# Weight pieces and converted blocks beside a linear attention, two turns later

## The chip, the core and the metric

The kernel runs on one core of a Trainium2 chip. The metric is the device time of one execution in microseconds, as a median of several runs. A core has five engines that each take their own instructions in order: TensorE (PE; its weight loads are listed as PEld), VectorE (DVE), ScalarE (ACT), GpSimd (POOL) and SyncE (SP), which here issues the loads and stores. They meet by semaphores: an instruction that waits holds everything behind it on its engine.

## The reference

Three layers follow one another; the sizes are batch 4, 8 heads, 768 tokens, head size 64. The first is a linear attention with decay in blocks, with a state that is carried from block to block:

```python
intra = np.einsum('bhic,bhjc->bhij', qb, kb) * Dmask[None]
intra = np.einsum('bhij,bhjd->bhid', intra, vb)
inter = np.einsum('bhid,bhde->bhie', qb * lam_pow[None], kv_state)
out[:, :, sl] = intra + inter
kb_dec = kb * rev_pow[None]
kv_state = lam_block[None, :, None, None] * kv_state + np.einsum('bhsd,bhse->bhde', kb_dec, vb)
```

The second is a soft mixture of 8 experts with 4 slots each: logits `x @ phi`, a softmax over all 3072 tokens that gathers the slots' inputs, `relu(slot @ w1[e]) @ w2[e]` for each expert (w1 512 x 1024, w2 1024 x 512, in float32), and a softmax over the slots that hands the results back. The third is a dense layer whose weights come as float64:

```python
h = x @ w_in
g = h * (1.0 / (1.0 + np.exp(-1.702 * h)))
return (g @ w_out).astype(np.float32)
```

## The kernel before, in words

**Turns.** The attention is cut into 32 steps: 4 batches, 2 halves of 384 tokens, 4 pairs of heads. A loop runs `for i in range(-2, NSTEP)`, and its order of instructions is the order on each engine, written out by hand. Turn i works on several steps at once: the scores of step i+1 (`do_SC`, tile bs, L293; VectorE multiplies them by the decay, L296), the transposes of q and k of step i+2 (`do_T`, tiles bq and bk, copied by ScalarE to qT, L265, and kT, L268), the transposes of the result of step i-1 (`do_XT`, tile bt, L351), the states' part of the result (`do_XS`, bx, L332), the state updates of step i+1 (`do_ST`, bst by TensorE at L306, then sa and s3 by VectorE at L315 and L317), the decayed k of step i+2 (`do_kd`, L281) and the rest of the result (`do_XA`, L340, copied by ScalarE to xT, L343). Then come the loads, and last GpSimd's product qdT of step i+2 (`do_qd`, L274). The step's updates are two or three pairs, for the last half of a batch has one chunk less. Beside each group of four turns stands the softmax tail of the group before (lines 360 to 473), so the turns differ in length. In this text turn i of the trace begins with the scores that the loop issues in turn i.

**Buffers.** qT and kT have one buffer each, but for a few steps at the ends. So the copy into qT of a step waits until the scores and GpSimd's product of the step before have read it.

**Expert pieces.** The first 32 pieces of w1 and w2, of 512 KB, are loaded beside the attention by `load_pieces(i)` (DMA issues at L155 and L157), the others after it as pieces are used up. All of these loads, those of q, k and v too, stand in SP's one queue in the order of the program.

**Blocks of float64.** Ten blocks of w_in and w_out, 128 x 256 numbers of 8 bytes, are turned into float32 beside the attention: `load_early(c)` loads block c into the only buffer `stage` (L221), and `do_early(c)` converts it: absolute values by ScalarE (L176), three bit operations by VectorE (L185, L188, L191), and two operations by GpSimd (L198, L199), of which the second reads what the third of VectorE leaves. EVERY is 2, so a block is loaded and one converted in every second turn.

**After the attention** come the experts (to about 194 us of the span) and a long stage of matrix products (bo, L986) to the end.

Of the kernel before, what the change touches and what calls it, by code (L numbers as in the profile page):

```python
# [17 lines left out]
def attention_moe_gelu_kernel(  # L18
# [31 lines left out]
    NSTEP = NG * NHP  # L50
    NE = 1
    NPC = 32
# [55 lines left out]
    def step_of(s):  # L108
        g, hp = divmod(s, NHP)
        b, hf = divmod(g, NHF)  # L110
        return b, hf, hp, g

    def load_step(s, what="qkv"):
        if s >= NSTEP:
            return
        b, hf, hp, g = step_of(s)
        t0 = hf * HS
        if "q" in what:

            q_r[s] = early.tile([P, 2, R * D], F32, tag="qr", name="qr", bufs=3)  # L120
            SP.dma_start(out=q_r[s], in_=q[b, 2 * hp:2 * hp + 2, t0:t0 + HS, :].rearrange("h (p c) d -> p h (c d)", p=P))
        for src, nm, ts, bufs, pool in ((k, "k", k_t, 3, early), (v, "v", v_t, 3, attn)):
            if nm in what:
                t = pool.tile([P, R, 2, D], F32, tag=nm, name=nm, bufs=bufs)
                for h in range(2):
                    SP.dma_start(out=t[:, :, h, :],
                                 in_=src[b, 2 * hp + h, t0:t0 + HS, :].rearrange("(c p) d -> p c d", p=P))
                ts[s] = t
# [17 lines left out]
    def load_piece(t=None):  # L146
        n = nxt_w[0]
        if n >= len(wlist):
            return
        nxt_w[0] += 1  # L150
        kind, e, j = wlist[n]
        if t is None:
            t = piece_room(n)
        if kind == "w1":
            SP.dma_start(out=t, in_=w1[e, j * P:(j + 1) * P, :])  # L155
        else:
            SP.dma_start(out=t.rearrange("p (k f) -> p k f", f=DM),  # L157
                         in_=w2[e, j * 2 * P:(j + 1) * 2 * P, :].rearrange("(k p) f -> p k f", p=P))
        w_pc[kind, e, j] = t
# [12 lines left out]
    def convert_abs(key, mask=None):  # L172
        if mask is None:
            mask = ex.tile([P, DM], F32, tag="cvm", name="cvm", bufs=3)
        m = mask
        ACT.activation(out=m, in_=staged[key][:, :, 1].bitcast(F32), func=AF.Abs)  # L176
        magn[key] = m

    def conversion(key, out, guard):


        t, m = staged.pop(key), magn.pop(key)
        up, low = t[:, :, 1], t[:, :, 0]
        a = out.bitcast(U32) if key[0] != "early" else stage[:, 2 * CB:3 * CB]
        DVE.tensor_scalar(out=a, in0=up, scalar1=3, scalar2=0x3FFFFFFF,  # L185
                          op0=ALU.logical_shift_left, op1=ALU.bitwise_and)
        yield
        DVE.scalar_tensor_tensor(out=a, in0=up, scalar=0xC0000000, in1=a,  # L188
                                 op0=ALU.bitwise_and, op1=ALU.bitwise_or)
        yield  # L190
        DVE.scalar_tensor_tensor(out=a, in0=low, scalar=29, in1=a,  # L191
                                 op0=ALU.logical_shift_right, op1=ALU.bitwise_or)
        yield
        if guard is DVE:
            DVE.scalar_tensor_tensor(out=out, in0=m, scalar=F64_MIN, in1=a.bitcast(F32),
                                     op0=ALU.is_ge, op1=ALU.mult)
        else:
            POOL.tensor_scalar(out=m, in0=m, scalar1=F64_MIN, scalar2=None, op0=ALU.is_ge)  # L198
            POOL.tensor_tensor(out=out, in0=a.bitcast(F32), in1=m, op=ALU.mult)  # L199

    def by_turns(*work, rounds=9):

        work = list(work)
        while work and rounds:
            work = [w for w in work if next(w, 0) is None]
            rounds -= 1
        return work
# [6 lines left out]
    EARLY = [(w_in32, kk * P, n * 512 + h * CB, w_in_sb[n][:, kk, h * CB:(h + 1) * CB])  # L214
             for n in range(NE) for kk in range(KD) for h in range(NCW)]
    EARLY += [(w_out32, 0, h * CB, wo[0][:, h * CB:(h + 1) * CB]) for h in range(NCW)]
    EVERY = (NSTEP - 8) // len(EARLY)
# [6 lines left out]
    def do_early(c):  # L224
        o = EARLY[c][-1]
        convert_abs(("early", c), o)
        by_turns(conversion(("early", c), o, POOL))
# [49 lines left out]
    def do_kd(s):  # L277
        b, hf, hp, g = step_of(s)
        t = early.tile([P, R, 2, D], F32, tag="kd", name="kd", bufs=1)
        for h in range(2):  # L280
            ACT.activation(out=t[:, :, h, :], in_=k_t[s][:, :, h, :], func=AF.Copy,  # L281
                           scale=dec[:, 2 * hp + h, P - 1:P])
        kd[s] = t
# [191 lines left out]
    with tc.manual_schedule():  # L475
# [7 lines left out]
        def warm_up(n):  # L483
            for _ in range(n):
                PE.matmul(bwarm, warm[:, :P], warm, start=True, stop=True)
# [17 lines left out]
        n = 1  # L503
# [12 lines left out]
        def make_isum():  # L516
            for j in range(G):
                for i in range(G):
                    POOL.tensor_copy(out=isum4[i * NS:(i + 1) * NS, j, :],
                                     in_=ident[i * NS:(i + 1) * NS, i * NS:(i + 1) * NS])  # L520

        def load_pieces(i):
            n = min(NPC, (i + 3) * NPC // NSTEP, NPC - 1 if i < NSTEP - 5 else NPC)
            while nxt_w[0] < n:
                load_piece()

        for i in range(-2, NSTEP):
            g, ph = divmod(i, NHP)
            if i > -2:
                load_step(i + 5, "q")  # L530
            if i == 1:
                make_isum()

            if 0 <= i + 1 < NSTEP:
                do_SC(i + 1)
            if 0 < i + 2 < NHP:

                for h in range(2):
                    make_dec(2 * (i + 2) + h)

            if 0 <= i + 2 < NSTEP:
                do_T(i + 2)
                if i == -2:
                    warm_up(1)
            if 0 <= i - 1 < NSTEP:
                do_XT(i - 1)
            if 0 <= i + 3 < NSTEP:
                do_q(i + 3)
            if ph == 1 and 0 <= g - 1 < NG:
                tail_L(g - 1)  # L550
            if ph == 2 and 0 <= g - 1 < NG:
                tail_max(g - 1)
            if ph == 3 and 0 <= g - 1 < NG:
                tail_exp(g - 1)
            if i == NSTEP - 1:
                tail_logits_first(NG - 1)
            if 0 <= i < NSTEP:
                do_XS(i)

            if 0 <= i + 1 < NSTEP:  # L560
                do_ST(i + 1)
            if 0 <= i + 2 < NSTEP:
                do_kd(i + 2)
            if 0 <= i < NSTEP:
                do_XA(i)

            if ph == 0 and 0 <= g - 1 < NG:
                tail_logits(g - 1)
            if ph == 0 and 0 <= g - 2 < NG:
                tail_z(g - 2, "tk")  # L570
                tail_slot(g - 2)
                tail_acc(g - 2)
            if i == NSTEP - 4:
                load_pieces(i + 1)

            load_pieces(i)

            load_step(i + 5, "k")
            c, turn = divmod(i - 2, EVERY)
            if turn == 1 and 0 <= c + 1 < len(EARLY):  # L580
                load_early(c + 1)
            if i >= 0:
                load_step(i + 3, "v")
            if 0 <= i + 2 < NSTEP:
                do_qd(i + 2)
            if i == -2:
                load_step(2, "v")
                SP.dma_start(out=phi_sb, in_=phi.rearrange("(k p) s -> p k s", p=P))
            if turn == 0 and 0 <= c < len(EARLY):
                do_early(c)  # L590
            if ph == 3 and 0 <= g - 1 < NG and i < NSTEP - 1:
                tail_row(g - 1)
            if ph == 0 and 0 <= g - 2 < NG:
                tail_row_exp(g - 2)
            if i == NSTEP - 2:
                early_cm.__exit__(None, None, None)
                slotb_cm = tc.tile_pool(name="slotb", bufs=NPC_B, side="right", reuse_waits="tile")
                slotb = slotb_cm.__enter__()

                rooms = [piece_room(NPC + j) for j in reversed(range(NPC_B))]  # L600
                while rooms:
                    load_piece(rooms.pop())
            if i == NSTEP - 1:
                attn_cm.__exit__(None, None, None)
                slotc_cm = tc.tile_pool(name="slotc", bufs=NPC_C, side="left", reuse_waits="tile")
                slotc = slotc_cm.__enter__()
                for _ in range(NPC_C):
                    load_piece()
# [498 lines left out]
```

## Time and profile before

| | |
|---|---|
| median of 3 runs | 501.6 us (501.26 to 502.44) |
| profiled execution | 501.21 us |
| its span | 499.1 us |
| TensorE busy | 485.1 us, 97% of the span |
| VectorE busy | 275.9 us, 55% |
| ScalarE busy | 273.8 us, 55% |
| GpSimd busy | 62.9 us, 13% |
| largest line: bo, L986 | 49% of the chain that ended last |
| DMA moved | 76.18 MB |

The span is what the profiler saw from the first instruction to the last; 2.1 us of the execution lie around it. Busy times are shares of the whole span, while the change lies in its first 160 us, so the rows below are read there. In the slices of the page the DMA engines are 0.8 to 0.9 busy or more over the attention, then fall.

### The profile page before, as it was taken

How to read it: one execution, taken by the hardware profiler on the slowest of the kernel's cores; microseconds unless marked ns; L12 is line 12 of the kernel's file. 1: busy time of each engine (PE TensorE's matmuls, PEld its weight loads, DVE VectorE, ACT ScalarE, POOL GpSimd, SP SyncE). 2: the span in 40 equal slices, each digit the busy share in tenths (PEclk: the TensorE clock that was granted, in tenths of full speed). 3: DMA queues.
4: the chain of work that ended last, by engine and by line, in shares of the span. 5: the costliest groups of instructions: out<-in, count | busy, mean ns of one | idle time of the engine just before them, and what ended most of it. 6: DMA issues, size and time to landing. Idle time of an engine off the chain costs nothing.

```text
span 499.1 us, 9454 instructions
## 1 busy us (share of the span) xinstructions
PE 485.1 (97%) x3561; PEld 380.1 (76%) x3561; DVE 275.9 (55%) x616; ACT 273.8 (55%) x569; POOL 62.9 (13%) x109
## 2 busy tenths in 40 slices
PE   8799999999999999999999999999999999999997
PEld 5688868778876436777777788888888888888886
DVE  5667878888874114897799895322152223322122
ACT  6577677687754335785866765434433443334432
POOL 3444354352221000000000000000000000000000
PEclk9999999999999999999999999999999999999999
DMA  8999989999989996353254220300020001200003
GB/s 199 295 276 287 278 242 289 274 276 269 259 271 330 376 395 266 122 167 129 76 177 154 101 84 1 126 1 0 1 101 25 1 1 46 82 1 0 1 0 126
DMA packets 82860, 76.18 MB, mean 153 GB/s; under 512 B 54400, under 2 KB 62848, under 8 KB 82816
## 3 DMA queue, kind: packets, MB, share of 16 engines
q1 hardware_dynamic: 82672, 75.58, 48.5%
q8 instruction: 28, 0.46, 0.4%
q14 instruction: 16, 0.13, 0.1%
q10 hardware_dynamic: 144, 0.00, 0.0%
HBM read 69.28 MB, written 6.29 MB: 151 GB/s over the span
## 4 chain that ended last, share of the span: by engine, by line
PE 81%; DVE 9%; DMA 6%; ACT 2%; issue 1%; DVEq 0%
PE bo L986 49%; PE bhh L939 4%; PE bs L293 4%; DMA stage<-in_moe_w_in_dram 4%; PE bacc L765 3%; PE bh L743 3%; PE bx L340 3%; PE bx L332 2%; PE bq L255 2%; PE bst L306 2%; PE bt L351 1%; DVE AT L296 1%; PE bk L257 1%; DMA v<-in_v_dram 1%; PE bl L361 1%
## 5 line engine op out<-in xcount | busy, mean ns | idle before, releaser
L986 PE MATMUL bo<-wlo,ghi 128*128 128x512 f32 x382 | 149.9, 394 | 1.1 <-DVE wlo L781 1.0
L986 PE MATMUL bo<-whi,glo 128*128 128x512 f32 x382 | 149.9, 394 | 0.0
L986 PE MATMUL bo<-whi,ghi 128*128 128x512 f32 x382 | 148.8, 391 | 0.1
L953 DVE TENSOR_TENSOR glo<-g,ghi 128x768 fp32r<-128x768 f32 x64 | 61.3, 957 | 134.6 <-ACT ghi L950 134.5
L947 ACT ACTIVATE g<-bhh 128x384 f32<-128x384 f32 x128 | 55.8, 488 | 122.2 <-PE bhh L939 119.2
L986 PEld LDWEIGHTS bo<-wlo,ghi 128*128 128x128 f32 x382 | 71.6, 188 | 18.0 <-issue 2.5
L986 PEld LDWEIGHTS bo<-whi,glo 128*128 128x128 f32 x382 | 71.7, 188 | 15.6 <-DVE glo L953 0.3
L986 PEld LDWEIGHTS bo<-whi,ghi 128*128 128x128 f32 x382 | 71.7, 188 | 14.1 <-DVE W2s L898 0.5
L950 ACT ACTIVATE ghi<-g 128x768 fp32r<-128x768 f32 (+1 forms) x65 | 54.3, 836 | 2.1
L274 POOL TENSOR_TENSOR qdT<-qT,qtab 128x384 f32<-128x384 f32 x32 | 32.2, 1007 | 39.6 <-PE bx L332 21.0
L293 PEld LDWEIGHTS bs<-qT,kT 64*128 64x128 f32 x384 | 25.9, 191 | 12.7 <-DVE zsum L453 4.2
L939 PE MATMUL bhh<-cT,W2s 128*128 128x384 f32 x128 | 33.6, 339 | 1.2 <-ACT w2raw L921 1.2
L293 PE MATMUL bs<-qT,kT 64*128 64x128 f32 x384 | 32.4, 294 | 1.6 <-DVE AT L296 0.9
L296 DVE TENSOR_TENSOR AT<-bs,dec 128x384 f32<-128x384 f32 x64 | 32.5, 549 | 2.0 <-PE bs L293 1.3
L265 ACT ACTIVATE qT<-bq 128x384 f32<-128x384 f32 x32 | 22.6, 705 | 13.8 <-PE bq L255 13.2
L939 PEld LDWEIGHTS bhh<-cT,W2s 128*128 128x128 f32 x128 | 23.9, 188 | 7.5 <-ACT w2raw L921 2.1
L281 ACT ACTIVATE kd<-k,dec 128x192 f32<-128x192 f32 x64 | 25.5, 446 | 5.2 <-issue 2.3
L340 PE MATMUL bx<-AT,v 128*64 128x128 f32 x384 | 27.2, 273 | 0.0
L176 ACT ACTIVATE cvm<-f 128x512 f32<-128x512 f32 x27 | 17.8, 666 | 8.2 <-DMA f<-in_moe_w_in_dram 6.4
L340 PEld LDWEIGHTS bx<-AT,v 128*64 128x64 f32 x384 | 21.0, 137 | 0.1
L306 PE MATMUL bst<-v,kd 128*64 128x64 f32 x320 | 17.4, 232 | 3.8 <-DMA v<-in_v_dram 2.9
L332 PE MATMUL bx<-qdT,sa 128*128 128x128 f32 x128 | 19.8, 277 | 0.0
(171 smaller groups left out, 598.7 us busy)
## 6 DMA issues: line engine op xcount, KB each, us to landing
w<-in_moe_w_dram SPq DMA_DIRECT2D x64, 512.0 KB, 5.9
f<-in_moe_w_out_dram SPq DMA_DIRECT2D x15, 512.0 KB, 3.2
qr<-in_q_dram SPq DMA_DIRECT2D x32, 192.0 KB, 4.2
k<-in_k_dram SPq DMA_DIRECT2D x64, 96.0 KB, 4.2
v<-in_v_dram SPq DMA_DIRECT2D x64, 96.0 KB, 4.0
f<-in_moe_w_in_dram SPq DMA_DIRECT2D x12, 512.0 KB, 3.9
out_dram<-o SPq DMA_DIRECT2D x23, 256.0 KB, 2.1
stage<-in_moe_w_in_dram SPq DMA_DIRECT2D x8, 256.0 KB, 4.4
```

The costliest lines, as they stand in the source:

```text
L274: POOL.tensor_tensor(out=qdT[s], in0=qT[s].rearrange("m (c i) -> m c i", c=R), in1=qtab[:, hp, None, :].to_broadcast([P, R, P]), op=ALU.mult)
L281: ACT.activation(out=t[:, :, h, :], in_=k_t[s][:, :, h, :], func=AF.Copy, scale=dec[:, 2 * hp + h, P - 1:P])
L293: PE.matmul(bs[h][:, cs], kT[s][hs, cs], qT[s][hs, cs], start=True, stop=True)
L296: DVE.tensor_tensor(out=t, in0=bs[h][:, :HS].rearrange("m (c i) -> m c i", c=R), in1=dec[:, 2 * hp + h, None, :].to_broadcast([P, R, P]), ...
L306: PE.matmul(bst[h * D:(h + 1) * D, c * D:(c + 1) * D], kd[s][:, c, h, :], v_t[s][:, c, h, :], start=True, stop=True)
L332: PE.matmul(bx[:, c * P:(c + 1) * P], state(s, first + c), qdT[s][:, c, :], start=(c == chunks[0]), stop=False)
L340: PE.matmul(bx[h * D:(h + 1) * D, c * P:(c + 1) * P], v_t[s][:, c, h, :], AT[s, h][:, c, :], start=False, stop=(c == R - 1))
L939: PE.matmul(bh[j][u][:, :HS], W2s[:, f * P:(f + 1) * P], cT[tg // (NTG // 2)][:, t0:t0 + HS], start=True, stop=True)
L947: ACT.activation(out=g[j][:, u * HS:(u + 1) * HS], in_=bh[j][u][:, :HS], func=AF.Gelu_apprx_sigmoid)
L950: ACT.activation(out=ghi[j][:, o], in_=g[j][:, o], func=AF.Copy)
L953: DVE.tensor_tensor(out=glo[j][:, o], in0=g[j][:, o], in1=ghi[j][:, o].bitcast(F32), op=ALU.subtract)
L986: PE.matmul(ob[t], a[j][:, t * P:(t + 1) * P], w[f], start=(begin and i == 0), stop=(end and i == 2))
```

## The change

The diff has two parts.

The first is in the table of expert pieces. Before, after turn i at most (i + 3) * 32 // 32 pieces are loaded, so the first at turn -2. Now it is max(0, i + 1) * 32 // 31, so the first at turn 0. Counted from 0, turn 28 now issues pieces 28 and 29, where before it issued 30 and 31; turn 29 issues none, and pieces 30 and 31 stand in turn 30 right ahead of the five pieces of the next pool.

The second is in the conversions. `do_early(c)` stood at the end of turn 2c + 2; it now stands in turn 2c + 3, after `do_kd` and ahead of `do_XA`. The load of block c stays in turn 2c + 1, after k's load and ahead of v's; it now comes behind the conversion of block c - 1 in the same turn.

```diff
--- before.py
+++ after.py
@@ -520,7 +520,7 @@
                                      in_=ident[i * NS:(i + 1) * NS, i * NS:(i + 1) * NS])
 
         def load_pieces(i):
-            n = min(NPC, (i + 3) * NPC // NSTEP, NPC - 1 if i < NSTEP - 5 else NPC)
+            n = min(NPC, max(0, i + 1) * NPC // (NSTEP - 1), NPC - 1 if i < NSTEP - 5 else NPC)
             while nxt_w[0] < n:
                 load_piece()
 
@@ -561,6 +561,10 @@
                 do_ST(i + 1)
             if 0 <= i + 2 < NSTEP:
                 do_kd(i + 2)
+
+            c, turn = divmod(i - 3, EVERY)
+            if turn == 0 and 0 <= c < len(EARLY):
+                do_early(c)
             if 0 <= i < NSTEP:
                 do_XA(i)
 
@@ -576,8 +580,7 @@
             load_pieces(i)
 
             load_step(i + 5, "k")
-            c, turn = divmod(i - 2, EVERY)
-            if turn == 1 and 0 <= c + 1 < len(EARLY):
+            if turn == 0 and 0 <= c + 1 < len(EARLY):
                 load_early(c + 1)
             if i >= 0:
                 load_step(i + 3, "v")
@@ -586,8 +589,6 @@
             if i == -2:
                 load_step(2, "v")
                 SP.dma_start(out=phi_sb, in_=phi.rearrange("(k p) s -> p k s", p=P))
-            if turn == 0 and 0 <= c < len(EARLY):
-                do_early(c)
             if ph == 3 and 0 <= g - 1 < NG and i < NSTEP - 1:
                 tail_row(g - 1)
             if ph == 0 and 0 <= g - 2 < NG:
```

On ScalarE, around the first conversion (turns 2 to 4; w_in0 is the block's place, its name for all blocks here), before:

```order
L343 ACTIVATE xT_473<-bx_448 128x384
L176 ACTIVATE w_in0_102<-stage_103 128x256
L265 ACTIVATE qT_513<-bq_505 128x3x128
L268 ACTIVATE kT_515<-bk_506 128x384
L352 ACTIVATE xn_369<-bt_517 128x3x128
L246 ACTIVATE q_522<-qr_325 128x2x3x64
L281 ACTIVATE kd_536<-k_317,dec_80 128x3x64 x2
L343 ACTIVATE xT_545<-bx_524 128x384
L265 ACTIVATE qT_580<-bq_572 128x3x128
```

and now:

```order
L343 ACTIVATE xT_469<-bx_444 128x384
L265 ACTIVATE qT_503<-bq_495 128x3x128
L268 ACTIVATE kT_505<-bk_496 128x384
L352 ACTIVATE xn_365<-bt_507 128x3x128
L246 ACTIVATE q_512<-qr_321 128x2x3x64
L281 ACTIVATE kd_526<-k_313,dec_80 128x3x64 x2
L176 ACTIVATE w_in0_102<-stage_103 128x256
L343 ACTIVATE xT_541<-bx_514 128x384
L265 ACTIVATE qT_576<-bq_568 128x3x128
```

The block's L176 stood behind the copy xT of turn 2 and ahead of the copies qT and kT of turn 3. Now it stands behind the kd of turn 3 and ahead of the xT of that turn. The bit operations of VectorE moved in the same way, behind turn 3's state updates.

On GpSimd at the same place, before:

```order
L274 TENSOR_TENSOR qdT_483<-qT_437,qtab_81 128x384
L198 TENSOR_SCALAR w_in0_102<-w_in0_102 128x256
L199 TENSOR_TENSOR w_in0_102<-stage_103,w_in0_102 128x256
L274 TENSOR_TENSOR qdT_556<-qT_513,qtab_81 128x384
L274 TENSOR_TENSOR qdT_630<-qT_580,qtab_81 128x384
```

and now:

```order
L274 TENSOR_TENSOR qdT_479<-qT_433,qtab_81 128x384
L198 TENSOR_SCALAR w_in0_102<-w_in0_102 128x256
L199 TENSOR_TENSOR w_in0_102<-stage_103,w_in0_102 128x256
L274 TENSOR_TENSOR qdT_552<-qT_503,qtab_81 128x384
L274 TENSOR_TENSOR qdT_626<-qT_576,qtab_81 128x384
```

Here nothing moved: L198 and L199 of the first block stand, before and now, between the products qdT that turns 2 and 3 issue.

## Rows read from the trace of the kernel before

**Rows 1.** Waits of the first 160 us: engine, line, awaited, total us, times, longest.
```profile
ACT w_in L176 <- DMA stage<-in_moe_w_in_dram: 12.0, 8, 2.5
```

**Rows 2.** Timeline, undisturbed turns: start us, us, engine, line, operation, idle before.
```profile
130.36 0.72 ACT L265 ACTIVATE qT<-bq 128x384 f32<-128x384 f32 x1 [0.83 <-PE bq L255]
...
132.56 0.94 PE L293 MATMUL bs<-qT,kT 64*128 64x128 f32 x12
...
132.78 0.47 ACT L343 ACTIVATE xT<-bx 128x384 f32<-128x384 f32 x1
...
134.07 0.71 ACT L265 ACTIVATE qT<-bq 128x384 f32<-128x384 f32 x1 [0.83 <-PE bq L255]
...
134.61 0.49 ACT L268 ACTIVATE kT<-bk 128x384 f32<-128x384 f32 x1
...
135.45 1.01 POOL L274 TENSOR_TENSOR qdT<-qT,qtab 128x384 f32<-128x384 f32 x1 [2.83 <-PE bx L332]
...
136.27 0.94 PE L293 MATMUL bs<-qT,kT 64*128 64x128 f32 x12
...
137.79 0.70 ACT L265 ACTIVATE qT<-bq 128x384 f32<-128x384 f32 x1 [0.57 <-POOL ra L461]
...
137.85 0.49 PE L351 MATMUL bt<-ident,xT 128*128 128x128 f32 x3
...
139.44 0.59 DVE L317 SCALAR_TENSOR_TENSOR sa<-s,qtab,bst 64x64 f32<-64x64 f32 x2 [1.16 <-PE bst L306]
...
140.07 0.59 DVE L317 SCALAR_TENSOR_TENSOR sa<-sa,qtab,bst 64x64 f32<-64x64 f32 x2
...
141.68 0.94 PE L293 MATMUL bs<-qT,kT 64*128 64x128 f32 x12
```

**Rows 3.** Timeline of one conversion and the product qdT behind it.
```profile
44.42 0.29 DVE L185 TENSOR_SCALAR stage<-stage 128x256 uint32<-128x256 uint32 x1 [2.48 <-DMA stage<-in_moe_w_in_dram]
...
44.87 1.01 POOL L198 TENSOR_SCALAR w_in<-w_in 128x256 f32<-128x256 f32 x1 [3.42 <-ACT w_in L176]
...
45.21 0.51 DVE L191 SCALAR_TENSOR_TENSOR stage<-stage 128x256 uint32<-128x256 uint32 x1
...
46.65 1.00 POOL L274 TENSOR_TENSOR qdT<-qT,qtab 128x384 f32<-128x384 f32 x1
```

**Rows 4.** Timeline, the tail's two reductions.
```profile
144.19 0.56 DVE L372 TENSOR_REDUCE L<-bL 128x96 f32<-128x384 f32 x1
...
144.78 0.60 DVE L374 TENSOR_REDUCE cm<-L 128x128 f32<-128x384 f32 x1
```

**Rows 5.** Timeline of turn 2: scores, load of v, states.
```profile
16.59 0.94 PE L293 MATMUL bs<-qT,kT 64*128 64x128 f32 x12
...
17.54 1.26 SPq L126 DMA_DIRECT2D v<-in_v_dram  x2
...
22.46 0.77 PE L306 MATMUL bst<-v,kd 128*64 128x64 f32 x11 [1.95 <-DMA v<-in_v_dram]
```

**Rows 6.** Windows: PE, PEld, DVE, ACT, POOL busy us; PEclk, DMA share, GB/s.
```profile
20.00:30.00 10.00, 8.05 (x88) 6.89 (x87) 4.94 (x16) 5.73 (x14) 3.64 (x4) 0.83 1.07 290
...
60.00:70.00 10.00, 8.80 (x108) 7.17 (x109) 7.44 (x24) 6.96 (x19) 4.05 (x5) 1.00 0.93 263
...
140.00:150.00 10.00, 9.41 (x119) 7.29 (x117) 7.80 (x25) 5.01 (x12) 1.51 (x3) 1.00 0.77 264
...
170.00:180.00 10.00, 10.00 (x128) 4.09 (x120) 1.41 (x6) 2.65 (x6) 0.62 (x2) 1.00 1.04 398
```

**Rows 7.** Timeline, qT copies of turns 4 and 22, next scores.
```profile
30.43 0.69 ACT L265 ACTIVATE qT<-bq 128x384 f32<-128x384 f32 x1 [0.82 <-PE bq L255]
...
113.26 0.70 ACT L265 ACTIVATE qT<-bq 128x384 f32<-128x384 f32 x1 [0.99 <-PE bq L255]
...
115.57 0.94 PE L293 MATMUL bs<-qT,kT 64*128 64x128 f32 x12
```

**Rows 8.** Source view, line 157 (w2 pieces): who waited, us, times.
```profile
  PEld bacc L765: 0.2, 1
```

## The prediction

> **What bounds the kernel now.** I read the page's slices first, then the waits of the first 160 us, then the timeline turn by turn. The second half is a matrix stage that the change does not touch, so the question is what one turn of the attention loop waits for. In the waits the reader is to see that ScalarE stood 12.0 us before the absolute values of a block (L176), until that block's load had landed [rows 1]. The load is issued one turn ahead and lands after that turn has ended. ScalarE and VectorE work in order, so the copies of q and k behind L176 stand too.
>
> A turn, counted from its scores (bs), takes 3.71 us (132.56 to 136.27) or, with the tail's slot work, 5.41 (to 141.68) [rows 2]. In an undisturbed turn the reader is to see how much room the other steps have. GpSimd's product qdT ends at 136.46 (135.45 + 1.01). The next copy into qT, which has one buffer and must wait until qdT has read it, starts at 137.79: 1.33 of room. The kT behind it ends at 135.10 (134.61 + 0.49) in the turn before, and the scores start at 136.27: 1.17 of room. So qdT may come 1.3 us late before ScalarE feels it, and 2.5 us late before TensorE does.
>
> **The change part by part.**
>
> *A. The opening.* Two of the 512 KB weight pieces leave the front of SP's queue. At 398 GB/s [rows 6] each is 1.3 us of the DMA engines. The v load of step 3 was issued behind them at 17.54 and TensorE, free from 20.51, stood 1.95 us for it, until 22.46 [rows 5]. 2.6 us earlier makes 19.9, in time; I allow 0.2 of lateness. The turn that began at 16.59 then takes 3.71, and turn 3 starts at 20.3 to 20.5; I take 20.4. The first conversion now runs in turn 3: the state updates (sa) start 3.17 after the scores (136.27 to 139.44) and take 1.22 (to 140.07 + 0.59) [rows 2]; the conversion takes 1.30 (44.42 to 45.21 + 0.51), and from its end to the end of qdT, with L199 between, it is 1.93 (to 46.65 + 1.00) [rows 3]. So the qT copy of turn 4 starts at 20.4 + 3.17 + 1.22 + 1.30 + 1.93 = 28.0, at the most 28.2, which I take, against 30.43 [rows 7]: **-2.2**. Bounds: -1.0 if only one piece's time comes through, -3.0 if turn 3's own tail is shorter.
>
> *B. The conversions, a turn later.* The L176 wait of 12.0 us goes: the block now has two turns to land. But what is late next? The order rows show that on ScalarE and VectorE the conversion moved to the end of the following turn, while on GpSimd its two instructions (L198, L199) still stand ahead of the same qdT. Before, a conversion ran at the start of the turn whose qdT stood behind it. Now qdT waits for L199, L199 for the last VectorE step, and that one for the state updates at the turn's end. Behind qdT the copy into qT waits, behind that all of ScalarE, and TensorE's scores wait for kT. This closes a ring of two turns, from one held qT copy to the next:
> - qT copy to the end of the copy xT, last on ScalarE in the even turn: 2.89 (130.36 to 132.78 + 0.47);
> - the transposes bt that need that xT, to the state updates: 1.59 (137.85 to 139.44);
> - state updates 1.22 for two chunks [all rows 2];
> - conversion 1.30, then L199 and qdT 1.93 [rows 3];
> - three handovers at 0.05.
>
> The sum is 9.1 us. Where the step's state has three chunks, a third pair of updates (0.59) makes it 9.7. In the turn after the tail's logits two reductions (0.56 and 0.60) stand ahead of the updates [rows 4], half of it beside TensorE's work: 9.65, and 10.15 with three chunks. From turn 4 to turn 22 there are nine rings, in the order 9.65, 9.7, 10.15, 9.1, 9.65, 9.7, 10.15, 9.1, 9.65: 86.9 us. In the trace the same stretch, from the qT copy of turn 4 to that of turn 22, took 113.26 - 30.43 = 82.8 [rows 7], with the L176 waits in it. So **+4.1**, which I round to +4.0. Bounds: the ring cannot be shorter than two turns of TensorE's own work, and three short turns to each long one make 16.54 for four, or 74 for the stretch: -8. From above, if every conversion's last step waited for all of L198 (45.88 instead of 45.21), 0.67 more nine times: +10. I take the ring's own sum, since each of its links is a row.
>
> *C. After the last conversion.* The scores of turn 23 start 1.1 behind the held qT copy (0.54 to kT, 0.49 for it), where the trace has 2.31 (113.26 to 115.57) [rows 2, 7]: -1.2. The bt of that turn then waits 0.2 for its xT: **-1.0**. Bounds -1.3 to 0.
>
> *D. TensorE's clock.* After the 1.95 us wait the granted clock fell to 1.2 GHz: the stretch 20 to 30 shows 0.83; 60 to 70, where TensorE was busy 8.80 of 10, shows 1.00 [rows 5, 6]. The opening's fall goes, and is in A. The ring makes waits of its own: after a ring of 9.65 or 10.15, TensorE is through with its two turns some 1.7 to 2.2 us early. I take one fall at **+0.7**; bounds 0 and, with five, +5.
>
> A page of the Trainium skill bears on this: TensorE: Matmul & The Clock Gate, What's actually happening, says that the slow clock is the default and activity lifts it. By that rule waits that return each group could bring it down each time; the trace has waits of more than 1 us with and without a fall, so I count one.
>
> *E. The end of the queue.* Pieces 30 and 31 now stand in turn 30 with the five of the next pool. In 140 to 150 the DMA engines were busy 0.77 of the time [rows 6], room for 2.3 us of the 2.6. Later TensorE stood 0.2 us for a w2 piece [rows 8], so those loads are just in time. I take **0**; bounds 0 and +2.6.
>
> *F. SP and DVE.* The load of the next block is now queued behind the conversion of the same turn, and v behind it. Within the ring the conversion ends some 7 to 8 us after the qT copy; v then lands before the ring after next asks for it. Nothing; up to +0.5 a ring if it does not. VectorE's work is the same in number.
>
> Sum: -2.2 + 4.0 - 1.0 + 0.7 = +1.5 on the profiled execution's 501.21 (span 499.1): 502.7. That execution lies 0.4 under the median of the three runs, 501.6, so I predict **503.1**.
>
> A rule that speaks about L198: SBUF, State Buffer (Who interferes with whom) in the Trainium skill says that a VectorE instruction with two SBUF inputs and a reading GpSimd instruction block each other wholly. Here L191 started at 45.21 and ended after 0.51 while L198 ran from 44.87 to 45.88 [rows 3], so the trace does not show a full block. By the rule the conversions would cost the 0.67 of B's upper end.
>
> **The rivals.**
> - *v takes the stage's place* (ends on the other side). If GpSimd's chain is shorter than I make it, the limit is the loads: v is issued right behind the block's load. Then the front's two pieces give 2.6 us and the rings some 2: 497. It decides where the ring falls under 8.9 us, that is, if L199 and qdT end within 1.7 us after the state updates instead of 3.2. v is not far from late even now: TensorE stood for it in the opening, and the DMA engines stay as full (0.93 in 60 to 70) [rows 5, 6]. Against it speaks that qdT stands behind L199 in the order.
> - *The two cancel.* A ring of 9.3 us on average gives +1 in B, and the gains of A and C then leave 499.5 to 502.6, no change that can be told. A short ring in the turns with two chunks speaks for it; the reductions and third chunks against.
> - *The waits cost more.* Five clock falls, or full blocks of L198: +4 to +6 beyond the sum, 508. The fall in the opening speaks for it, the full clock in 60 to 70 and 140 to 150 against it [rows 6].
> - *The change does not do what it says*: the block has not landed after two turns either. Its load waits for VectorE, but then has 8 us; I give it nothing of its own.
>
> **How the numbers follow.** The ring as computed: 0.55 (501 to 507, most of it slower). v in the stage's place: 0.20. Cancelled: 0.12. Costlier waits: 0.13. About 0.2%, 1 us, is what a measurement of this kernel can tell from no change. Faster gets the 0.20 and 0.05 of the ring's lower edge: 0.25; the same 0.17; slower 0.58. For 8 in 10 the range reaches from half of the faster case to the costlier waits: 498.8 to 508.5. The likeliest case's own range is 501 to 507.
>
> **What would show it.** Right: no wait of ScalarE for the block's load; ScalarE's qT copy released by GpSimd's qdT ten times, some 2.5 us each, 25 us in all; scores released by kT in every second odd turn; the qT copy of turn 4 near 28.2 and that of turn 22 near 115; TensorE's wait for v in turn 2 gone. C is wrong if turn 23 starts later than 1.5 us behind that copy, E if TensorE waits for w pieces over 1 us in all. The prediction is wrong if qT is released by TensorE's transposes (bq) in the conversion's turns, with v the longest wait of TensorE, or if the clock row shows 0.5 in most groups.

## The result and the profile after

The changed kernel takes 507.4 us as a median of 6 runs (506.8 to 509.48), the kernel before 501.36 in the runs beside it (497.76 to 502.44): a ratio of 1.0143, 95% interval 1.012 to 1.0167. It is slower by 6.0 us, where 1.5 was forecast. The profiled execution took 506.80 us with a span of 505.0.

The waits of the first 160 us (engine, line, awaited: us in total, times, longest) have no row for L176 any more, where 12.0 us stood before [rows 1]. In its place:

```profile
ACT qT L265 <- POOL qdT L274: 25.4, 9, 3.5
...
PE bs L293 <- ACT kT L268: 8.4, 8, 1.8
...
ACT qT L265 <- PE bl L361: 7.0, 2, 3.5
...
PEld bz L448 <- ACT kT L268: 4.9, 4, 1.8
...
PE bst L306 <- DMA v<-in_v_dram: 1.3, 3, 0.5
```

One of the nine waits for GpSimd's qdT, 0.85 us, is of turn 2, ahead of the first conversion. The two that the profile puts down to bl are waits for qdT as well: in turn 8 qdT ended 0.04 us ahead of the copy:

```profile
47.45 1.01 POOL L274 TENSOR_TENSOR qdT<-qT,qtab 128x384 f32<-128x384 f32 x1
...
48.50 0.68 ACT L265 ACTIVATE qT<-bq 128x384 f32<-128x384 f32 x1 [3.50 <-PE bl L361]
```

So ten copies into qT are held, those of turns 4 to 22, 31.5 us in all; ten and 25 us were forecast. In eight turns TensorE's scores stand for kT.

The timeline of the opening (answers to [rows 5, 7]) shows TensorE waiting for v in turn 3, the state updates behind it, and the first held copy, of turn 4:

```profile
24.10 0.39 PE L306 MATMUL bst<-v,kd 128*64 128x64 f32 x5 [0.53 <-DMA v<-in_v_dram]
...
24.59 0.59 DVE L317 SCALAR_TENSOR_TENSOR sa<-s,qtab,bst 64x64 f32<-64x64 f32 x2 [1.94 <-PE bst L306]
...
29.01 0.71 ACT L265 ACTIVATE qT<-bq 128x384 f32<-128x384 f32 x1 [2.88 <-POOL qdT L274]
```

Here is one ring, from the held copy of turn 20 to that of turn 22, ScalarE, VectorE and GpSimd (columns as in [rows 2]):

```profile
108.58 0.77 ACT L265 ACTIVATE qT<-bq 128x384 f32<-128x384 f32 x1 [2.77 <-POOL qdT L274]
...
111.02 0.51 ACT L343 ACTIVATE xT<-bx 128x384 f32<-128x384 f32 x1
...
111.76 0.32 ACT L467 ACTIVATE re<-ra 128x96 f32<-128x96 f32 x1
...
112.11 0.25 DVE L469 TENSOR_REDUCE rs<-re 128x3 f32<-128x96 f32 x1
...
112.69 0.99 DVE L296 TENSOR_TENSOR AT<-bs,dec 128x384 f32<-128x384 f32 x2
...
113.60 0.56 DVE L372 TENSOR_REDUCE L<-bL 128x96 f32<-128x384 f32 x1
...
114.71 0.58 DVE L317 SCALAR_TENSOR_TENSOR sa<-s,qtab,bst 64x64 f32<-64x64 f32 x2
...
115.85 0.85 POOL L198 TENSOR_SCALAR wo<-wo 128x256 f32<-128x256 f32 x1 [2.58 <-ACT wo L176]
...
115.95 0.45 DVE L185 TENSOR_SCALAR stage<-stage 128x256 uint32<-128x256 uint32 x1
...
116.43 0.42 DVE L188 SCALAR_TENSOR_TENSOR stage<-stage 128x256 uint32<-128x256 uint32 x1
...
116.89 0.42 DVE L191 SCALAR_TENSOR_TENSOR stage<-stage 128x256 uint32<-128x256 uint32 x1
...
117.46 0.73 POOL L199 TENSOR_TENSOR wo<-stage,wo 128x256 f32<-128x256 f32 x1 [0.76 <-DVE stage L191]
...
118.15 1.00 POOL L274 TENSOR_TENSOR qdT<-qT,qtab 128x384 f32<-128x384 f32 x1
...
119.18 0.68 ACT L265 ACTIVATE qT<-bq 128x384 f32<-128x384 f32 x1 [3.04 <-POOL qdT L274]
...
120.23 0.94 PE L293 MATMUL bs<-qT,kT 64*128 64x128 f32 x12 [1.21 <-ACT kT L268]
```

From rs at 112.11 on VectorE is hardly ever idle until the conversion's L191 has ended at 117.31; then come L199, qdT and the held copy. TensorE in the same ring:

```profile
110.04 0.21 PE L448 MATMUL bz<-ones,e 128*32 128x1 f32 x6
...
110.11 1.06 PE L433 MATMUL bp<-xn,e 128*32 128x512 f32 x6
...
111.10 0.94 PE L293 MATMUL bs<-qT,kT 64*128 64x128 f32 x12
...
112.68 0.49 PE L351 MATMUL bt<-ident,xT 128*128 128x128 f32 x3
...
113.00 0.49 PE L370 MATMUL bL<-ident,lp 128*128 128x128 f32 x3
```

bz writes the bank that kT's copy reads, so with the slot product bp it waits for the held kT. The scores of turn 21, then bt and bL follow; bL ends at 113.49, when VectorE is about to reduce it (L372 at 113.60).

At the end, TensorE's wait for the last expert pieces in 194 to 210 us (0.2 before, [rows 8]):

```profile
PEld bacc L766 <- DMA w<-in_moe_w_dram: 1.2, 2, 0.8
```

### The profile page after: what moved, and what is told of

Read it like the earlier page. It is cut to its first block, busy times and chain, and to the rows that moved or that the text cites. A ratio compares the mean times of both kernels' runs of the same rounds, so it can differ in the third digit from the quotient of the medians.

```text
span 505.0 us, 9436 instructions
## 1 busy us (share of the span) xinstructions
PE 483.7 (96%) x3561; PEld 376.4 (75%) x3561; DVE 276.4 (55%) x616; ACT 270.5 (54%) x569; POOL 61.6 (12%) x109
## 4 chain that ended last, share of the span: by engine, by line
PE 73%; DVE 9%; ACT 7%; DMA 5%; issue 3%; SPq 1%; POOL 1%; ACTq 0%; POOLq 0%; DVEq 0%
PE bo L987 46%; PE bhh L940 4%; PE bacc L766 3%; PE bh L744 3%; DMA v<-in_v_dram 2%; PE bx L340 2%; PE bs L293 2%; PE bx L332 2%; DMA k<-in_k_dram 2%; ACT kd L281 2%; PE bt L351 2%; PE bst L306 2%; DVE glo L954 1%; PE bq L255 1%; SPq L126 1%
## 5 line engine op out<-in xcount | busy, mean ns | idle before, releaser
L293 PE MATMUL bs<-qT,kT 64*128 64x128 f32 x384 | 30.0, 289 | 8.4 <-ACT kT L268 8.4
L293 PEld LDWEIGHTS bs<-qT,kT 64*128 64x128 f32 x384 | 23.9, 187 | 19.0 <-ACT kT L268 10.8
L176 ACT ACTIVATE cvm<-f 128x512 f32<-128x512 f32 x27 | 17.8, 667 | 8.6 <-DMA f<-in_moe_w_in_dram 5.3
L317 DVE SCALAR_TENSOR_TENSOR sa<-sa,qtab,bst 64x64 f32<-64x64 f32 x64 | 17.9, 280 | 2.1
```

What stands on the lines that cost most here:

```text
L293: PE.matmul(bs[h][:, cs], kT[s][hs, cs], qT[s][hs, cs], start=True, stop=True)
```

## The experiments

Ratios are against runs of the kernel before on the same chip (medians there 500.96 to 502.28). "Stretch" is the time from the qT copy of turn 4 to that of turn 22: 82.83 us before, 90.17 in the changed kernel.

**The two parts apart.** The pieces moved by two turns, the conversions by one. The new table of pieces on the kernel before:

```diff
-            n = min(NPC, (i + 3) * NPC // NSTEP, NPC - 1 if i < NSTEP - 5 else NPC)
+            n = min(NPC, max(0, i + 1) * NPC // (NSTEP - 1), NPC - 1 if i < NSTEP - 5 else NPC)
```

> The kernel before with the new table of expert pieces alone; the conversions stay at the end of turn 2c+2. Theory (the loss comes from conversions whose GpSimd part holds the copy into qT): the opening gains about 2 us, ScalarE's waits for the block's load stay at some 10 to 12 us in all, no qT copy waits over 1.5 us for qdT, and the end loses at most 0.5 us for the last piece: 497 to 501 us. Rival (the pieces carry the loss: two turns later they collide with the loads of the expert phase, so that TensorE waits for the last pieces): 503 us or more, with the loss after 150 us of the span.

Measured 498.70 us, ratio 0.9931 (0.9907 to 0.9955). The qT copy of turn 4 started at 28.25, 2.2 earlier than before; the stretch stayed at 82.83, with the waits for the block in it:

```profile
ACT w_in L176 <- DMA stage<-in_moe_w_in_dram: 12.1, 8, 2.7
...
PE bst L306 <- DMA v<-in_v_dram: 2.0, 2, 1.4
```

The conversions in their new place with the old table (the edit above taken back in the changed kernel):

> The changed kernel with the old table of expert pieces; the conversions stand in turn 2c+3. Theory: the ring of two turns is the same as in the changed kernel, so from the qT copy of turn 4 to that of turn 22 some 90 us, nine or ten copies held by qdT for about 25 us in all, and the opening waits for v as before the change: 507 to 511 us. Rival (pieces carry the loss): 500 to 503 us.

Measured 510.59 us, ratio 1.0166 (1.0144 to 1.0189), stretch 90.13. One row of its waits:

```profile
ACT qT L265 <- POOL qdT L274: 24.6, 9, 3.5
```

So the pieces win 3.6 us, and the moved conversions alone lose 8.3. The two do not quite add up to the 6.0 of both (they make 4.7); the kernel before's own medians, 500.96 to 502.28, differ by about as much from chip to chip. The rings are those of the changed kernel to within 0.1 us, whatever the pieces do.

**The link.** GpSimd's part of the conversion behind the product of the same turn:

```diff
-        by_turns(conversion(("early", c), o, POOL))
+        gp_part[c] = by_turns(conversion(("early", c), o, POOL), rounds=3)
...
             if 0 <= i + 2 < NSTEP:
                 do_qd(i + 2)
+            if turn == 0 and 0 <= c < len(EARLY):
+                by_turns(*gp_part.pop(c))
```

`rounds=3` issues VectorE's three steps (L185 to L191); the second call issues L198 and L199.

> The changed kernel with one thing moved: GpSimd's two instructions of a conversion (L198, L199) are issued behind the product qdT of the same turn instead of ahead of it; ScalarE's and VectorE's part stay where the change put them. Theory: no qT copy is held by qdT any more, scores wait for kT no more than 0.3 us, and the stretch from the qT copy of turn 4 to that of turn 22 falls from 90.2 us to 76 to 82: 493 to 499 us. Rival 1 (VectorE's conversion at the turn's end is late for the decay of the scores and ScalarE's copies by itself, whatever GpSimd's order): 504 us or more. Rival 2 (the DMA engines, full in this stretch, bound it): the stretch does not fall under 82 us, waits for v or the block take the place, 498 to 501 us.

A second buffer for qT, with room for it, and nothing moved:

```diff
-    for tag, n, bufs in (("kd", HS, 1), ("kT", HS, 1), ("qT", HS, 1), 
+    for tag, n, bufs in (("kd", HS, 1), ("kT", HS, 1), ("qT", HS, 2), 
...
-                return early.tile([P, HS], F32, tag=tag, name=tag, bufs=1)
+                return early.tile([P, HS], F32, tag=tag, name=tag, bufs=2 if tag == "qT" else 1)
```

> The changed kernel with a second buffer for qT, and nothing moved: L198 and L199 still stand ahead of qdT. Theory (qT's one buffer is the link between the late qdT and ScalarE): the copies into qT wait for TensorE's transposes again, the stretch from turn 4 to turn 22 is 76 to 82 us, 493 to 499 us, within 1 us of the kernel in which GpSimd's part is moved. Rival (the late qdT is itself what TensorE waits for, in the states' product bx): TensorE waits for qdT instead and the time stays at 504 us or more.

They took 498.72 us (0.9934, 0.9907 to 0.996) and 498.51 us (0.9927, 0.9907 to 0.9947). Waits of the first (its lines are two higher), then of the second:

```profile
ACT qT L267 <- PE bq L257: 20.9, 28, 1.0
...
PE bst L308 <- DMA v<-in_v_dram: 7.0, 8, 1.8
```

```profile
ACT qT L265 <- PE bq L255: 20.1, 28, 1.0
...
PE bst L306 <- DMA v<-in_v_dram: 2.2, 3, 1.6
```

The copies into qT are released by TensorE's transposes again, so either end of the link, GpSimd's order or qT's one buffer, carries the loss of some 9 us. That VectorE's later conversion is late by itself is out. With GpSimd moved, v takes the place, as the prediction's rival on the other side and rival 2 here had it: the stretch is 84.28, over the 76 to 82 of the theory, in an execution that was the slowest of its six (500.60). With two buffers it is 81.80, at the upper end.

**Why v is late.** The loads of v ahead of the block's load, in the kernel with GpSimd's part behind, in that with two buffers, and in the changed kernel alone:

```diff
+            if i >= 0:
+                load_step(i + 3, "v")
             if turn == 0 and 0 <= c + 1 < len(EARLY):
                 load_early(c + 1)
-            if i >= 0:
-                load_step(i + 3, "v")
```

> The kernel with GpSimd's part of the conversion behind qdT, and now the loads of v issued ahead of the block's load in the same turn. There TensorE waited some 13 us in all for v. Theory 1 (v is late since SP's queue stands at the block's load until the conversion has read the buffer, up to 1.4 us a time): the waits for v fall to under 5 us and the time to 493 to 496 us. Theory 2 (v is late since the DMA engines are full, whatever the order in the queue): waits move to other loads or stay, 497 to 500 us.

> The kernel with two buffers for qT, and the loads of v ahead of the block's load. Theory 1 (queue order makes v late): 494 to 497 us. Theory 2 (full DMA engines): 497 to 500 us, as with the block's load first.

> The changed kernel with the loads of v ahead of the block's load, and nothing else. Theory (the ring through L199, qdT and qT sets the time, loads do not): the nine copies of qT stay held, 24 to 26 us in all, and only the waits for v of turns 3 and 20, some 1 us, can go: 505.5 to 508 us. Rival (the late loads are part of the ring): 503 us or less.

In the first expectation the 13 us count one wait twice, as 7.0 on the matmuls and 6.3 on their weight loads; TensorE stood about 7 us. That kernel took 496.77 us (0.9908, 0.9876 to 0.9941), the fastest median of all, with a stretch of 80.52; its wait for v:

```profile
PE bst L308 <- DMA v<-in_v_dram: 1.6, 5, 0.4
```

The second took 497.29 (0.99, 0.9867 to 0.9934). Both medians lie past the upper end of what queue order alone promised (496 and 497), and the intervals overlap those of the kernels with the block's load first. In the first the waits for v did go; with two buffers they did not (3.3 us), so how much of v's lateness is the queue and how much the full DMA engines stays open. The third took 509.06 us (1.0136, 1.0104 to 1.0169), over the 505.5 to 508 expected. The copies stay held whatever the order of the loads, and the rings stay as they were but for two. In the ring 4 to 6 (10.32) v was now 1.2 us late. The waits:

```profile
ACT qT L265 <- POOL qdT L274: 25.4, 9, 3.5
```

In the ring 10 to 12 (10.16, 8.96 in the changed kernel) the granted clock fell after a wait of 1.77 us for kT, which ended at 61.21; the windows (columns as in [rows 6]):

```profile
62.00:64.00 2.00, 2.00 (x15) 1.66 (x12) 1.02 (x2) 1.91 (x6) 0.00 (x0) 0.64 0.73 257
...
64.00:66.00 2.00, 2.00 (x18) 1.77 (x19) 0.34 (x2) 1.20 (x5) 0.00 (x0) 0.50 0.83 185
...
66.00:68.00 2.00, 2.00 (x29) 1.71 (x26) 1.83 (x6) 1.47 (x4) 0.82 (x1) 1.00 0.94 258
```

**The rings that were longer than forecast.** The slot stage (bz, bp, zsum, acc) left out in turns 12, 16 and 20:

```diff
-            if ph == 0 and 0 <= g - 2 < NG:
+            if ph == 0 and 0 <= g - 2 < NG and g - 2 not in (1, 2, 3):
                 tail_z(g - 2, "tk")
```

> The changed kernel with the softmax tail's slot stage (products bz and bp, and the sums zsum and acc behind them) left out in turns 12, 16 and 20; in turn 8 it stays, as a control. The forecast put ScalarE's queue on the ring of two turns and had no slot stage in it; the changed kernel's rings that hold one took 10.85, 10.53, 10.86 and 10.60 us where 10.15, 9.65, 10.15 and 9.65 were forecast. Theory (TensorE's queue is on those rings: bz waits for the held kT, which has the bank it writes, and bp, the scores and the transposes follow before bt): the rings 12 to 14, 16 to 18 and 20 to 22 fall to 9.4 to 10.2 us, the ring 8 to 10 stays at 10.8, and the whole loses 2.2 to 3.5 us: 503 to 505 us. Rival (the excess lies in the conversion or in late loads): these rings stay at 10.4 us or more, 506 us or more.

Then the row step one turn later in the changed kernel, and both together:

```diff
-            if ph == 0 and 0 <= g - 2 < NG:
+            if ph == 1 and 0 <= g - 2 < NG:
                 tail_row_exp(g - 2)
```

> The changed kernel with the tail's row step (ScalarE's re, L467; VectorE's row sums and reciprocal, L469 to L472) one turn later: at the end of turns 9, 13, 17 and 21 in place of 8, 12, 16 and 20. The changed kernel's rings that pass these turns took 10.85, 10.53, 10.86 and 10.59 us, 0.7 to 0.9 above the forecast, and leaving out the slot stage did not shorten them. Theory A (two paths of the same length run through these turns, ScalarE's re with VectorE's row sums, and TensorE's slot stage, scores and transposes up to bL; the forecast had neither): moving the row step alone takes no more than 0.3 us off each ring, and the time stays at 506 to 508 us. Theory B (the row step alone is the excess): the four rings fall by 0.6 to 0.9 to 9.7 to 10.2 us, 503 to 505 us.

> As the kernel with the row step one turn later, and the slot stage (bz, bp, zsum, acc) of turns 12, 16 and 20 left out as well; that of turn 8 stays. Theory A (two paths of the same length): only now the rings 12 to 14, 16 to 18 and 20 to 22 fall, by 0.7 to 1.1 us each, to 9.5 to 10.0 us, and the ring 8 to 10 stays above 10.4 us; the time falls by 2 to 3.5 us to 503 to 505 us. Theory B (the row step alone): the same as with the row step moved alone, all four rings short. Theory C (neither, but VectorE's conversion or the loads): the rings stay at 10.4 us or more.

One run each: 507.43, 507.91 and 506.87 us. These times cannot be told from the changed kernel's 506.8 to 509.48, so only the rings are read. In us, by the turns of their qT copies:

| ring | forecast | changed | no slot stage | row step later | both |
|---|---|---|---|---|---|
| 4 to 6 | 9.65 | 9.55 | 9.57 | 10.11 | 9.74 |
| 6 to 8 | 9.70 | 9.94 | 9.94 | 9.94 | 9.94 |
| 8 to 10 | 10.15 | 10.85 | 10.86 | 11.21 | 11.21 |
| 10 to 12 | 9.10 | 8.96 | 8.95 | 8.95 | 10.17 (clock) |
| 12 to 14 | 9.65 | 10.53 | 10.51 | 10.55 | 9.56 |
| 14 to 16 | 9.70 | 9.94 | 11.13 (clock) | 9.94 | 9.95 |
| 16 to 18 | 10.15 | 10.86 | 10.98 | 10.85 | 9.88 |
| 18 to 20 | 9.10 | 8.95 | 8.95 | 8.96 | 8.96 |
| 20 to 22 | 9.65 | 10.59 | 10.51 | 10.56 | 9.55 |

My first theory, TensorE's slot stage alone, fell: without it the ring did not move. The last ring without the slot stage:

```profile
109.72 0.71 ACT L265 ACTIVATE qT<-bq 128x384 f32<-128x384 f32 x1 [2.77 <-POOL qdT L274]
...
110.80 0.94 PE L293 MATMUL bs<-qT,kT 64*128 64x128 f32 x12 [0.39 <-ACT kT L268]
...
113.17 0.25 DVE L469 TENSOR_REDUCE rs<-re 128x3 f32<-128x96 f32 x1 [2.94 <-ACT re L467]
...
120.22 0.68 ACT L265 ACTIVATE qT<-bq 128x384 f32<-128x384 f32 x1 [4.00 <-POOL qdT L274]
```

The scores come early, but VectorE stands 2.94 us for re. With the row step later (first) and with both edits (second):

```profile
109.52 0.71 ACT L265 ACTIVATE qT<-bq 128x384 f32<-128x384 f32 x1 [2.77 <-POOL qdT L274]
...
114.47 0.56 DVE L372 TENSOR_REDUCE L<-bL 128x96 f32<-128x384 f32 x1 [0.51 <-PE bL L370]
...
120.08 0.68 ACT L265 ACTIVATE qT<-bq 128x384 f32<-128x384 f32 x1 [2.88 <-POOL qdT L274]
```

```profile
109.98 0.71 ACT L265 ACTIVATE qT<-bq 128x384 f32<-128x384 f32 x1 [2.76 <-POOL qdT L274]
...
113.95 0.56 DVE L372 TENSOR_REDUCE L<-bL 128x96 f32<-128x384 f32 x1 [0.90 <-PE bL L370]
...
119.53 0.68 ACT L265 ACTIVATE qT<-bq 128x384 f32<-128x384 f32 x1 [2.87 <-POOL qdT L274]
```

Now bL releases L372. From the held copy to L372 it is 5.02 us in the changed kernel, 5.09 without the slot stage, 4.95 with the row step later, and 3.97 with both. So two paths of one length lie on these rings, and only taking both away brings the rings to 9.55 to 9.88. The last run's time missed the expected 503 to 505 all the same. Its three rings are shorter by 3.0 us together, but it opened 1.6 us later, lost 1.2 to a fall of the clock in its ring 10 to 12, and 0.6 in two other rings: in 4 to 6 v was 0.66 late, and in 8 to 10, with the row step one turn later, L199 started 0.36 later in its ring, behind VectorE's L470.

**The row step in the fastest kernel.**

> The fastest kernel so far (GpSimd's part behind qdT, loads of v ahead of the block's load, 496.8 us) with the row step one turn later. There no copy of qT is held, so no ring passes through the row step. Theory: no more than 1 us either way, 495.5 to 498 us. Rival (the row step delays TensorE's scores or transposes in those turns too): 493 to 495 us.

Measured 498.69 us, ratio 0.9942 (0.9921 to 0.9964), against 0.9908 without that edit: no gain, the median over the 495.5 to 498 expected, the intervals overlapping. By its median the version to keep is the one with GpSimd's part behind qdT and v ahead of the block's load; it beats both kernels. But its interval overlaps that of two buffers with v ahead (0.99) and that of the new table of pieces alone (0.9907 to 0.9955). So no run shows that moving the conversions gains anything beyond the pieces.

## Why the prediction was wrong in size

The mechanism and the sign were right, with the held copies, the kT waits and L176's wait gone as told. The size was not: by the spans +5.9 us and not +1.5. The 507.4 measured lies inside the wide range, next to the 508 of the rival *The waits cost more*, but that is luck: neither of that rival's causes, clock falls and full blocks of L198, is in the trace.

- **A, opening: -1.4 for -2.2.** Turn 3 started at 20.42, as worked out (20.4). But TensorE waited twice for the v of step 4, 0.86 in all; the state updates began at 24.59, 1.0 later than the sum had them. I had priced only the v of step 3. That v of step 4 stands behind the first block's load in SP's queue; in the fastest kernel, where it stands ahead, that wait was 0.36. With the pieces alone the copy of turn 4 did come 2.2 earlier, but by chance: there it waits for no late qdT, and v was 1.39 late in turn 3.
- **B, rings: +7.3 for +4.0, the step that failed.** The term that was too short is the ring's way from the held copy to the state updates. My ring went from the copy xT straight to bt and gave the tail half of two reductions. Where the turn holds the tail's slot stage and row step, in four of nine rings, there is more between the held copy and the state updates: lp, re, row sums and the decay on ScalarE and VectorE, and as long a path on TensorE. These four took 42.8 us where 39.6 were forecast; the other five took 47.3, as forecast. I had built the ring from a turn without that stage, although the chain that ended last in the kernel before ran through it, here in turns 8 and 12:

```profile
51.33 0.92 PE bp L433 x6
52.27 0.60 DVE acc L440
...
70.16 0.92 PE bp L433 x6
71.11 0.51 DVE acc L442
```

- **C: -0.9 for -1.0.** The scores of turn 23 start 1.05 after the held copy (120.23 against 119.18; 1.1 forecast).
- **D, clock: 0 for +0.7.** The profiled execution kept the granted clock at 1.00 over the attention, although TensorE waited up to 1.8 us. In an execution of a variant a wait of 1.77 us was followed by a fall, which cost a ring 1.2 us; in the kernel without the slot stage none followed the longest wait, 2.9 us.
- **E, the last pieces: +0.9 for 0**, inside its bound of 2.6, but wrong by its own sign: TensorE waited 1.2 us in all for w pieces, over the 1. It was 4.98 us late in turn 31, 5.50 late at the last piece, for which it waited, and 5.94 late at the first bo. The last piece itself was issued 6.1 late (188.5 us for 182.4). With the old table and the moved conversions TensorE waited as long for it (0.78 us, 0.84 here), so it is not the new table that makes it late; why the loads did not catch up as TensorE did in C stays open.
- **F: nothing**, as forecast. The conversion took 1.36 us (115.95 to 117.31; 1.21 to 1.44 over the ten) where 1.30 was forecast, so B's upper end did not come. The Trainium skill (SBUF, State Buffer, Who interferes with whom) has a VectorE instruction with two SBUF inputs contend with a GpSimd instruction that reads SBUF, under an exclusive lock. In the ring above L188 ran from 116.43 while L198 ran to 116.70, at 0.42 and 0.85, so the trace shows no full block. Some steps do get longer, by 0.1 to 0.2 us, for a reason that no run shows: L185 beside L198 took 0.45 there and 0.29 before [rows 3], and in turn 3 both L188 and L198 took longer than in that ring:

```profile
25.84 1.01 POOL L198 TENSOR_SCALAR w_in<-w_in 128x256 f32<-128x256 f32 x1 [5.57 <-ACT w_in L176]
...
26.16 0.51 DVE L188 SCALAR_TENSOR_TENSOR stage<-stage 128x256 uint32<-128x256 uint32 x1
```

-1.4 + 7.3 - 0.9 + 0.9 make the 5.9 of the spans.

Of the rivals, v in the stage's place is what remains once the ring is cut; it decided nothing here, since the ring is over 8.9 us everywhere. The rings average 10.0 us, so *The two cancel*, which asked for 9.3, is out too.

## What to carry to other kernels

When work moves to another time on two engines, look at the third that shares it: its place in that engine's order decides what is held, and a buffer that exists once hands the hold on. A ring must be summed over every stage that passes between its ends, in the turn where it passes; the chain that ended last in the profile before can name such stages. When two paths have one length, taking either away shows nothing; take both.

## What had not been expected

One fall of the granted clock to 1.2 GHz (0.50 in the window 64 to 66 above) cost the ring it fell in 1.2 us (10.16 for 8.96, and 11.13 for 9.94 in the kernel without the slot stage). SP, too, stands at the block's load until the conversion has read the buffer, 0.9 us in the median of the changed kernel's nine waits and 1.4 at most, with v behind it.
